# Making the x sums of a third unit of tokens in an earlier block of a fused attention and expert kernel

## The chip, the cores and the metric

One core of one Trainium2 chip. The time of a run is the device time of that core in microseconds (us), and each kernel has several runs. A profile is one execution seen by the hardware profiler; its span is about 1.7 us shorter than the time of the same execution.

## The reference, cut to what matters

Attention with cosine weights over 8 batches of 576 tokens gives x, 4608 tokens of 512 numbers. A gate matrix gives each token a weight for each of 8 experts, balanced by eight rounds of row and column sums. Each expert is a two-layer network.

```python
x = attn_out.transpose(0, 2, 1, 3).reshape(B * S, H * D)      # 4608 x 512
P = np.exp(x @ w_gate - ...)
for _ in range(8):
    P /= P.sum(1, keepdims=True); P /= P.sum(0, keepdims=True); P *= N / E
for e in range(8):
    out += P[:, e:e+1] * (np.maximum(x @ w1[e], 0) @ w2[e])
```

## The kernel before

Expert 0 runs in nine blocks of 512 tokens (block 0 to 8), mixed with the attention of the next batch. Experts 1 to 7 use a scheme of seven products in place of eight, on six units of 384 token pairs. It needs, for each unit, three sums of parts of x (S1, S2, S4) and one part of x replaced by a difference. The sums are made once and kept in DRAM; each later expert loads them again.

```python
def x_sums(n, ts):                       # unit n: four VectorE sums, three stores
    a11, a12, a21, a22 = (x_part(i, j, n) for i in range(2) for j in range(2))
    s1, s2, s4 = ts
    for out_, in0, in1, op in (
        (s1, a21, a22, ALU.add), (s2, s1, a11, ALU.subtract),
        (s4, a12, s2, ALU.subtract), (a21, a11, a21, ALU.subtract),
    ):
        ve.tensor_tensor(out=out_, in0=in0, in1=in1, op=op)
        yield
    for i, t in enumerate(ts):
        saved.append(nc.sync.dma_start(out=x_saved[n, i], in_=t...))
```

The first two units' sums are made in block 6, in tiles that the attention no longer needs (three of the k_p tiles, three of the q_p tiles); the others in expert 1, one unit ahead of their use. After block 6 the attention's tiles are given up, and H, the hidden layer's tile, takes their room. Block 7 writes into H first:

```python
for j in range(B - 1, NJ):               # blocks 7 and 8
    hT = next_h()                        # a half of H
    ...
            ffn1(hT, w0, j, [slot])      # 4 matmuls into h_ps (two buffers),
                                         # then ScalarE: relu into hT
            if j == B - 1 and slot == 0:
                gates(B - 1, Z[:])       # ScalarE: exp, start of the balancing
```

At the start of unit 1 of expert 1, two rows of the result are weighted on GpSimd:

```python
            if e == 1 and n == 0:
                ...
                w2_first(w)
                for _ in range(2):
                    gate(ungated.pop(0), nc.gpsimd)
```

Of the kernel before, what the change touches and what calls it, by code (L numbers as in the profile page):

```python
# [25 lines left out]
def kernel(  # L26
# [13 lines left out]
    B, H, S, D = q.shape  # L40
# [41 lines left out]
    def not_before(earlier, i):  # L82

        if earlier is not None:
            tc.add_manual_dep(
                i.ins,
                earlier.ins.name,
                mybir.DependencyInfo(mybir.DependencyClass.NoSync, mybir.DependencyReason.DATA),
                reason="written order",
            )  # L90
# [29 lines left out]
    def new_weights(pool):  # L120
        return pool.tile([P, KT, F], F16, name="w1e"), pool.tile([P, FT, Dm], F16, name="w2e")

    def load_w1(w, e, cuts, parts=None):
        view = moe_w1[e].rearrange("(kt p) f -> p kt f", p=P)
        for i in range(cuts) if parts is None else parts:
            f0, f1 = i * F // cuts, (i + 1) * F // cuts
            nc.gpsimd.dma_start(out=w[0][:, :, f0:f1], in_=view[:, :, f0:f1])

    def load_w2(w, e, cuts):
        view = moe_w2[e].rearrange("(ft p) d -> p ft d", p=P)  # L130
        for i in range(cuts):
            f0, f1 = i * FT // cuts, (i + 1) * FT // cuts
            nc.gpsimd.dma_start(out=w[1][:, f0:f1, :], in_=view[:, f0:f1, :])
# [61 lines left out]
    def x_sums(n, ts):  # L195
# [10 lines that stand above are left out]
            saved.append(  # L206
                nc.sync.dma_start(out=x_saved[n, i], in_=t.rearrange("p k t -> p (k t)"))
            )

    saved = []  # L210

    with ExitStack() as p1:
        ld = p1.enter_context(tc.tile_pool(name="ld", bufs=4))
        kp_pool = p1.enter_context(tc.tile_pool(name="kp_pool", bufs=4))
        qp_pool = p1.enter_context(tc.tile_pool(name="qp_pool", bufs=3))
# [419 lines left out]
        def at(block, slot, fn, *args):  # L635
            todo.setdefault((block, slot), []).append((fn, args))
# [150 lines left out]
                for half in range(2):  # L787
                    at(j, 11 + half, load, b + 2, half, "qkv", True)
        def x_sums_early(n):
            pool, name = ((kp_pool, "k_p"), (qp_pool, "q_p"))[n]  # L790
            ts = [pool.tile([P, C, 2, D], F16, name=name) for _ in range(3)]
            for _ in x_sums(n, [
                t[:].rearrange("p c a d -> p (c a d)")[:, 0 : KH * TU].rearrange(
                    "p (k t) -> p k t", k=KH
                ) for t in ts
            ]):
                pass

        for n in range(2):
            at(B - 2, (2, 5)[n], x_sums_early, n)  # L800

        y_pss = {}
        for j in range(B - 1):
# [43 lines left out]
    def next_h():  # L847
        nonlocal turns_h
        turns_h += 1
        return H[:, turns_h % 2]  # L850
# [9 lines left out]
    def x_tiles():  # L860
        return [s2_pool.tile([P, KH, TU], F16, name=name) for name in ("S1", "S2", "S4")]

    def x_again(n, ts, earlier=None):
        for i, t in enumerate(ts):
            not_before(earlier, nc.sync.dma_start(
                out=t[:].rearrange("p k t -> p (k t)"), in_=x_saved[n, i]
            ))

    def w1_sums(w, i):
        tw, steps = w1_steps(w, i)  # L870
        for step in steps:
            step()
        return tw
# [42 lines left out]
    def group(hT, tw, xs, n, i, fill):  # L916

        b11, T1, b21, b22, T2, T3, T4 = tw
        s1, s2, s4 = (t[:] for t in xs)
        h11, h12 = hT[:, i, 0:TU], hT[:, FH + i, 0:TU]  # L920
        h21, h22 = hT[:, i, TU : 2 * TU], hT[:, FH + i, TU : 2 * TU]
        X = ps_h[0].tile([P, TCH], FP32, name="h_ps")
        product(X, b11, x_part(0, 0, n), True)
        se.copy(out=Y[:, 0:TU], in_=X[:, 0:TU])  # L924
        fill()
        for fn in late:
            fn()
        late.clear()
        fill()
        product(X, T2, s2, False)  # L930
        u2 = snapshot(X, "u2")
        fill()
        product(Y, b21, x_part(0, 1, n), False)
        se.activation(out=h11, in_=Y[:, 0:TU], func=AF.Relu)  # L934
        fill()
        product(X, T1, s1, False)
        u4 = snapshot(X, "u4")
        fill()
        product(Z, T3, x_part(1, 0, n), True)
        add_relu(h22, Z, u4)  # L940
        fill()
        product(X, b22, s4, False)
        se.activation(out=h12, in_=X[:, 0:TU], func=AF.Relu)  # L943
        fill()

        def last():
            product(Z, T4, x_part(1, 1, n), False)
            add_relu(h21, Z, u2)

        late.append(last)  # L950
# [106 lines left out]
    def w2_first(w):  # L1057
        b11, b12 = w[1][:, 0:FH, 0:DH], w[1][:, 0:FH, DH:Dm]
        i = ve.tensor_tensor(out=b12, in0=b12, in1=b11, op=ALU.subtract)
        if ve is nc.vector:  # L1060
            not_before(latest, i)

    def mark(bank):

        te.matmul(
            out=bank, lhsT=xT[:, 0, 0:P], rhs=xT[:, 0, 0:TCH], start=True, stop=True,
            skip_group_check=True,
        )
# [55 lines left out]
    def gate(g, pool=None):  # L1124

        if pool is None:
            bound[2].mul(out=acc(g), in_=acc(g), mul=P_tok[:, g, 0:1])
        else:
            pool.tensor_scalar(
                out=acc(g), in0=acc(g), scalar1=P_tok[:, g, 0:1], scalar2=None, op0=ALU.mult,  # L1130
            )
# [12 lines left out]
    xs_first = [x_tiles() for _ in range(2)]  # L1144
    xs_next = xs_first[0]
# [64 lines left out]
    for e in range(1, E):  # L1210
        if e == 2:
            se = nc.scalar
        w = w_next
        for n in range(NU):
            hT = next_h()
            xs = xs_next
            for i in range(FH):
                group(hT, tws[i], xs, n, i, start_fill if e == 1 and n == 0 else pair_fill)
                m = (n + 1) % NU
                if e == 1 and m:  # L1220

                    if n == 0:
                        xs_next = xs_first[1]
                        continue
                    if i == 0:
                        xs_next = x_tiles()
                        sums_x = x_sums(m, [t[:] for t in xs_next])
                    next(sums_x)
                    if i == FH - 1:
                        next(sums_x, None)  # L1230
                elif i == 1:
                    xs_next = x_tiles()
                    if not (e == E - 1 and m == 0):
                        x_again(m, xs_next)

                if e > 1 and n == 0 and i == 0:
                    tws[FH - 1] = w1_sums(w, FH - 1)
                if e + 1 < E and n == NU - 1:
                    if i:
                        tws[i - 1] = w1_sums(w_next, i - 1)  # L1240
                    else:
                        w2_first(w_next)
            if e == 1 and n == 0:
                k_fill = 0
                for _ in balance:
                    pass
                mark(W2[:])
# [3 lines that stand above are left out]
                ve = nc.vector  # L1251
            if n == 0 and e + 1 < E:
                w_next = new_weights(wA if e % 2 else wB)
                load_w1(w_next, e + 1, 1)
            if n == 2 and e + 1 < E:
                load_w2(w_next, e + 1, 1)
            add_pairs(hT, e, w, n)
    for fn in late:
        fn()
    while stream:  # L1260
        _, pair, name = stream.pop(0)
# [32 lines left out]
```

## Time and profile before

| | us |
|---|---|
| median of 3 runs | 975.6 (975.55 to 975.99) |
| span of the profiled execution | 972.1 |
| TensorE busy | 959.4 |
| first group of block 7 starts at | 161.53 |
| from there to the end | 810.6 |

The profiled execution took 973.9 us, less than any of the three timed ones. How the views are read is told in the prediction, which shows their lines.

### The profile page before, as it was taken

What the parts mean: (1) busy time and instruction counts of PE and PEld (TensorE: products, weight loads), DVE (VectorE), ACT (ScalarE), POOL (GpSimd) and SP (SyncE); (2) the same over time, 40 slices, a digit from 0 to 9 for tenths busy, and PEclk for the clock granted to TensorE, in tenths of its full rate; (3) what the DMA queues carried; (4) which work ended last, traced back from release to release, by engine and by line L of the source; (5) the groups of instructions that cost most, each with busy time, mean ns of one, the idle gap of its engine ahead of it and who ended that gap; (6) DMA issues with size and microseconds to landing.
All of it is one profiled execution on the core that took longest, in us unless ns stands there. A gap on an engine that the chain in (4) does not pass through costs nothing.

```text
span 972.1 us, 20258 instructions
## 1 busy us (share of the span) xinstructions
PE 959.4 (99%) x7855; PEld 674.6 (69%) x7855; DVE 807.4 (83%) x1831; ACT 565.0 (58%) x1264; POOL 60.7 (6%) x82
## 2 busy tenths in 40 slices
PE   9999999999999999999999999999999999999997
PEld 6545555567777777777777777777777777777775
DVE  7767776789898887987888987987888987987887
ACT  5767665577776555555555555555555555555551
POOL 6231210010000000000000000000000000000001
PEclk9999999999999999999999999999999999999999
DMA  9999988231004301332004301322004401115435
GB/s 162 188 154 173 156 137 184 44 69 50 26 26 93 69 25 50 68 62 57 25 26 93 69 25 51 68 54 65 26 25 86 75 25 42 33 28 124 123 90 127
DMA packets 81200, 74.72 MB, mean 77 GB/s; under 512 B 33360, under 2 KB 73040, under 8 KB 81104
## 3 DMA queue, kind: packets, MB, share of 16 engines
q0 software_dynamic: 27232, 30.94, 20.4%
q1 hardware_dynamic: 53632, 42.24, 17.8%
q8 instruction: 61, 1.00, 0.4%
q14 instruction: 35, 0.29, 0.1%
q10 hardware_dynamic: 240, 0.26, 0.1%
HBM read 84.30 MB, written 12.98 MB: 100 GB/s over the span
## 4 chain that ended last, share of the span: by engine, by line
PE 91%; DMA 4%; issue 2%; DVE 1%; POOL 1%; ACT 0%; POOLq 0%; DVEq 0%; SPq 0%; ACTq 0%
PE rows_ps L109 34%; PE h_ps L109 28%; PE p_ps L109 11%; PE copied_ps L109 11%; PE y_ps L109 4%; PE small_ps L109 3%; DMA k_ld<-in_k_dram 1%; DMA w1e<-in_moe_w_dram 1%; DMA w2e<-in_moe_w_dram 1%; DVE acc_hi L975 0%; POOL q_ld L233 0%; POOL hs_last L990 0%; DMA out_dram<-acc_lo 0%; DVE H L905 0%; DVE S L203 0%
## 5 line engine op out<-in xcount | busy, mean ns | idle before, releaser
L975 DVE SCALAR_TENSOR_TENSOR acc_lo<-rows_ps,P_tok,acc_lo 128x512 f32<-128x512 f32 (+1 forms) x322 | 203.8, 642 | 74.9 <-PE rows_ps L109 74.8
L109 PEld LDWEIGHTS <-H 128*128 128x128 f16 x2080 | 203.1, 98 | 82.3 <-issue 1.4
L911 ACT CAST u<-h_ps 128x384 f16<-128x384 f32 x288 | 137.5, 478 | 129.7 <-PE h_ps L109 129.7
L109 PEld LDWEIGHTS <-w1e 128*128 128x128 f16 x1632 | 157.7, 98 | 67.2 <-issue 5.3
L905 DVE CUSTOM_DVE_ANT_0 H<-p_ps,u 128x384 f16<-128x384 f32 x329 | 181.7, 552 | 7.2 <-PE p_ps L109 7.1
L109 PEld LDWEIGHTS <-hs 128*128 128x128 f16 x1500 | 146.6, 98 | 56.2
L109 PE MATMUL p_ps<-xT,T 128*128 128x384 f16 x672 | 164.2, 326 | 1.0 <-DVE H L905 0.9
L109 PE MATMUL h_ps<-S,w1e 128*128 128x384 f16 x672 | 164.2, 326 | 0.8 <-ACT u L911 0.6
L109 PE MATMUL rows_ps<-V,H 128*128 128x256 f16 x1000 | 150.0, 273 | 0.7 <-DVE acc_hi L975 0.7
L109 PE MATMUL rows_ps<-w2e,hs 128*128 128x256 f16 x1000 | 150.0, 273 | 0.0
L109 PE MATMUL h_ps<-xT,w1e 128*128 128x384 f16 (+1 forms) x616 | 148.8, 351 | 0.1
L943 ACT ACTIVATE H<-h_ps 128x384 f16<-128x384 f32 x144 | 70.6, 490 | 94.5 <-PE h_ps L109 94.5
L109 PEld LDWEIGHTS <-T 128*128 128x128 f16 x1008 | 98.4, 98 | 31.9 <-issue 4.9
L109 PE MATMUL rows_ps<-w2e,H 128*128 128x256 f16 (+1 forms) x568 | 94.4, 285 | 0.0
L924 ACT COPY copied_ps<-h_ps 128x384 f32<-128x384 f32 x144 | 67.5, 469 | 36.0 <-PE h_ps L109 35.2
L934 ACT ACTIVATE H<-copied_ps 128x384 f16<-128x384 f32 x144 | 70.8, 492 | 20.4 <-PE copied_ps L109 20.4
L109 PE MATMUL h_ps<-S,T 128*128 128x384 f16 x336 | 81.8, 325 | 0.6 <-ACT copied_ps L109 0.5
L109 PE MATMUL copied_ps<-xT,w1e 128*128 128x384 f16 x336 | 82.1, 326 | 0.0
L109 PE MATMUL copied_ps<-w2e,H 128*128 128x256 f16 x504 | 75.6, 273 | 0.0
L109 PE MATMUL rows_ps<-V,hs 128*128 128x256 f16 x500 | 75.0, 273 | 0.0
L975 DVE SCALAR_TENSOR_TENSOR acc_lo<-copied_ps,P_tok,acc_lo 128x256 f32<-128x256 f32 x126 | 60.3, 479 | 0.4
L975 DVE SCALAR_TENSOR_TENSOR acc_hi<-rows_ps,P_tok,acc_hi 128x512 f32<-128x512 f32 (+1 forms) x56 | 41.4, 739 | 20.6 <-PE rows_ps L109 19.7
(146 smaller groups left out, 947.7 us busy)
## 6 DMA issues: line engine op xcount, KB each, us to landing
S<-x_saved SPq DMA_DIRECT2D x114, 192.0 KB, 2.4
out_dram<-acc_lo SPq DMA_DIRECT2D x62, 128.0 KB, 2.4
w1e<-in_moe_w_dram POOLq DMA_DIRECT2D x7, 1024.0 KB, 8.8
w2e<-in_moe_w_dram POOLq DMA_DIRECT2D x7, 1024.0 KB, 9.6
q_ld<-in_q_dram POOLq DMA_DIRECT2D x16, 288.0 KB, 6.5
k_ld<-in_k_dram POOLq DMA_DIRECT2D x16, 288.0 KB, 7.8
v_ld<-in_v_dram POOLq DMA_DIRECT2D x16, 288.0 KB, 9.6
x_saved<-S SPq DMA_DIRECT2D x12, 192.0 KB, 1.8
```

The lines of the kernel that those rows point to most:

```text
L109: i = getattr(self.engine, name)(*args, **kwargs)
L905: latest = ve._custom_dve(TENSOR_ADD_SAT, out=out, in0=ps[:, 0:TU], in1=t[:], s0=FP32_MAX, s1=0.0)
L911: se.copy(out=t[:], in_=ps[:, 0:TU])
L924: se.copy(out=Y[:, 0:TU], in_=X[:, 0:TU])
L934: se.activation(out=h11, in_=Y[:, 0:TU], func=AF.Relu)
L943: se.activation(out=h12, in_=X[:, 0:TU], func=AF.Relu)
L975: ve.scalar_tensor_tensor(out=a, in0=rows, scalar=P_tok[:, g, self.e : self.e + 1], in1=a, op0=ALU.mult, op1=ALU.add,)
```

## The change

Its intent: VectorE is backed up at the start of unit 1 of expert 1, where three of the four sums of the third unit stand in its queue, and idle for 3 us at the end of block 6. So the third unit's sums are made there too, stored, and loaded in expert 1 like the others.

```diff
-            pool, name = ((kp_pool, "k_p"), (qp_pool, "q_p"))[n]
+            pool, name = ((kp_pool, "k_p"), (qp_pool, "q_p"))[n % 2]
             ts = [pool.tile([P, C, 2, D], F16, name=name) for _ in range(3)]
...
-        for n in range(2):
-            at(B - 2, (2, 5)[n], x_sums_early, n)
+        for n in range(3):
+            at(B - 2, (2, 5, 9)[n], x_sums_early, n)
...
-                if e == 1 and m:
-                    if n == 0:
-                        xs_next = xs_first[1]
-                        continue
+                if e == 1 and n == 0:
+                    xs_next = xs_first[1]
+                    continue
+                if e == 1 and m > 2:
                     if i == 0:
                         xs_next = x_tiles()
...
-                        x_again(m, xs_next)
+                        x_again(m, xs_next, saved[-1] if e == 1 and m == 2 else None)
```

## The prediction

The forecast's sum is 975.6 - 0.5 + 3.1 = 978.2 us. Passages of the recorded text that no trace or run of this case shows are cut where it is marked; they are general statements (among them that a sum could be made no cheaper, which was not shown), and no term of the sum is among them.

> **What bounds the kernel now.** I read the page first, its busy times and its chain, to see which engine sets the time:
>
> ```profile
> PE 959.4 (99%) x7855; PEld 674.6 (69%) x7855; DVE 807.4 (83%) x1831; ACT 565.0 (58%) x1264; POOL 60.7 (6%) x82
> ...
> PE 91%; DMA 4%; issue 2%; DVE 1%; POOL 1%; ACT 0%; POOLq 0%; DVEq 0%; SPq 0%; ACTq 0%
> ```
>
> TensorE works 959.4 of 972.1 us and is 91% of the chain. So VectorE work has no price of its own: it costs or saves only where TensorE stands still for it. The order of instructions of the built program (not run) shows that TensorE's own order is the same, instruction by instruction, before and after. The question is only which TensorE waits go and which come. The waits of TensorE between 160 and 206 us, the stretch from block 7 to the second unit of expert 1, which are all that the change can touch:
>
> ```profile
> PE p_ps L109 <- DVE H L905: 0.9, 1, 0.9
> PE h_ps L109 <- ACT copied_ps L109: 0.5, 1, 0.5
> ```
>
> (From 206 to 300 us the same view has one wait of 0.6 us, for ScalarE.) The first line is the intended prize. The timeline of VectorE and TensorE there (start, duration, engine, operation):
>
> ```profile
> 198.91 0.74 DVE L203 TENSOR_TENSOR S<-xT 128x768 f16<-128x768 f16 x1 [0.46 <-PE h_ps L109]
> 199.69 0.56 DVE L203 TENSOR_TENSOR S<-S,xT 128x768 f16<-128x768 f16 x1
> 200.17 0.55 DVE L109 CUSTOM_DVE_ANT_0 H<-p_ps,u 128x384 f16<-128x384 f32 x1
> ...
> 201.28 0.55 DVE L203 TENSOR_TENSOR S<-xT,S 128x768 f16<-128x768 f16 x1
> ...
> 202.34 0.54 DVE L905 CUSTOM_DVE_ANT_0 H<-p_ps,u 128x384 f16<-128x384 f32 x1
> ...
> 205.02 0.55 DVE L905 CUSTOM_DVE_ANT_0 H<-p_ps,u 128x384 f16<-128x384 f32 x1
> ```
>
> VectorE is backed up; three of the four x sums of the third unit (L203, into S) stand in the queue, and the H at 205.02 lets TensorE go on only at 205.62.
>
> Now the place that receives the work, the end of block 6. VectorE there:
>
> ```profile
> 159.64 1.55 DVE L109 TENSOR_TENSOR xT<-small_ps,rb 128x384 f16<-128x384 f32 x4 [3.12 <-PE small_ps L109]
> ```
>
> An idle of 3.12 us, large enough for four sums. But the stores that follow the sums must land as well. The queue of stores and loads, and what it waits for:
>
> ```profile
> 152.37 1.51 SPq L207 DMA_DIRECT2D x_saved<-q_p  x3
> 162.62 2.76 SPq L865 DMA_DIRECT2D S<-x_saved  x6
> ```
>
> ```profile
> SPq L865 <- DMA x_saved<-q_p: 8.6, 2, 7.4
> ```
>
> The reloads wait for the stores of the second unit to land. Landing times, the instructions that touch q_p between 152.3 and 153.9 us:
>
> ```profile
> L207 SPq DMA_DIRECT2D x_saved<-q_p x3: 319/320/320, 152.4 to 153.6; - x3
> ...
> DMA to landing us min/median/max: 7.5/8.3/8.9
> ```
>
> So the last store, issued at 153.6, lands at 153.56 + 8.9 = 162.5. ScalarE's first write into the new tile H:
>
> ```profile
> 162.67 0.60 ACT L109 ACTIVATE H<-h_ps 128x512 f16<-128x512 f32 x1 [0.35 <-PE h_ps L109]
> ```
>
> It starts 0.2 us after that landing. The view names TensorE, whose matmuls (161.53, 1.03 us long) ended at 162.56, but it could not have started much earlier for the store either.
>
> [...] 768 columns take 0.55 us and the 1152-column products of the same kind 0.75, that is 384 more columns in 0.20 us, 1.9 a nanosecond. [...]
> [...] the six stores, issued from 147.9 to 153.6, land one after another, the last four at 158.6, 159.9, 161.2 and 162.5 (issue plus landing delay, same view for each), 1.3 us apart, while the weight loads of expert 1, issued at 147.15 and 147.90, run beside them. A store without that company (at 199.7 us) takes 1.9 us.
> [...]
>
> **The change part by part.**
> Removed in expert 1, unit 1: four sums (three of them before 205 us), three stores. I walked the new VectorE order with the old durations, from start to next start. The reciprocal and the gate product end at 198.46 as before. H (p_ps ready at 199.45) starts at 199.45 instead of 200.17; then its own 0.47, w2e 0.65, V 0.68, acc_hi 0.59 bring the H of 202.34 to 201.85. Up to the next H stand V, hs, V, H and hs, 0.47 + 0.61 + 0.33 + 0.61 + 0.33 + 0.34 = 2.69 later, at 204.54 instead of 205.02: the new order puts another V between, so of the 1.9 us removed only 0.48 reach this H. TensorE's wait shrinks from 0.85 to about 0.4. After that point TensorE has no wait for VectorE to lose. Saved: 0.5 us.
>
> Added in block 6: four sums of 0.59 + 0.59 + 0.48 + 0.46 = 2.1 us from 156.55 to 158.7 in the idle that lasts until 159.64. Two of them need k_p buffers that the stores of the first unit read, landed at 153.8 and 157.0; the sum that needs the second starts at about 157.7. No cost on VectorE.
>
> Added: three stores of 192 KB, issued at about 157.2, 157.8 and 158.4, in the same ring behind the q_p stores, of which the last lands at 162.5. In the built program, ScalarE's first write into H waits, before and after, for all stores out of k_p and q_p, because H takes their room in SBUF; after, the wait's counts include the three new stores. At 1.28 us each they land at about 163.8, 165.1 and 166.3; I take 166.1, since the weight load ends meanwhile and the ring then has the engines to itself.
> The write into H then starts at 166.1 + 0.15 = 166.25 instead of 162.67. TensorE can run two groups ahead, for h_ps has two buffers. The third group starts at 163.76 now (within 162.89 and 1.89 for eight matmuls) and would start when the first buffer is free, 166.25 + 0.6 = 166.85. New TensorE wait: 3.1 us. Nothing later gives it back, TensorE being busy to the end.
> Also added: three reloads in unit 1 of expert 1, some 15 us before their use; hidden. The six reloads of the first two units move from 162.6 into the time after the stores and land by about 171, needed at about 185.9; hidden.
>
> Sum: 975.6 - 0.5 + 3.1 = 978.2 us.
>
> **The rivals.**
> A: the stores land in time and the intended saving stands alone: 975.1 us. For it: VectorE has room, and unhindered stores take 1.9 us. Against: the measured 7.5 to 8.9 us for stores issued just before into the same ring.
> B: the new stores share bandwidth better than I think, because the bulk of the q_p stores is through by 161 us and only stragglers land at 162.5. Then the third lands at about 165.0, the wait is 2.0 us, the time 977.1.
> C: the stores slow the load of w2 so far that it or the reloads hold up unit 0 of expert 1. It lands 17.4 us after 147.9, at 165.3; its use is at 200. There are 35 us of room: no change of the time.
> D: the Sinkhorn chain slips. ScalarE's exponentials for it stand just behind the write into H, so they move by 3.6 us while TensorE moves by 3.1; the chain has 0.9 us before TensorE needs its first column sums (ready 165.45, used 166.34). It holds, but narrowly; at worst some 0.5 us more.
> E: removing sums helps all of unit 1 by their full 2.1 us: 973.5. Against: TensorE waits for VectorE there once, for 0.85 us.
>
> **Range and chances.** The mechanism (a wait for the new stores) is in the program; its size hangs on the third landing, between 165.0 (B) and 167. That gives 977.1 to 979.1, with some room below for A: 976.4 to 979.2. Two per cent would be 19.5 us, far outside all of this.
>
> **What would show it.** Right: a TensorE wait of about 3 us in the group h_ps at 163.8, put down to ScalarE (or ScalarE idle about 3.5 us before its first H), with the last x_saved<-k_p landing at about 166; the wait at 205.6, shifted, at about 0.4. Wrong: stores out of k_p landing before 163.5, no such wait, and a time below 975.6; or a wait of 0.85 gone entirely, which would make my walk of the VectorE order too pessimistic.

## The result, and the profile after

| | before | after |
|---|---|---|
| median, us | 975.63 (975.55 to 975.99, 4 runs) | 983.46 (980.55 to 984.02, 4 runs) |
| span of the profile | 972.1 | 981.2 |
| first group of block 7 | 161.53 | 163.76 |
| from there to the end | 810.6 | 817.4 |

The ratio of the fast runs is 1.0074 (95% interval 1.0053 to 1.0094): within 2%, but slower, and outside the predicted range. A ratio here is the mean time of one kernel's fast runs over the mean of the other's in the same rounds, so not quite the ratio of the medians.

The busy times and the chain of the page of the kernel after, which answer to the first lines of the prediction:

```profile
PE 963.5 (98%) x7855; PEld 676.0 (69%) x7855; DVE 807.6 (82%) x1831; ACT 565.3 (58%) x1264; POOL 61.1 (6%) x82
...
PE 90%; DMA 4%; DVE 3%; ACT 1%; issue 1%; POOL 1%; SPq 0%; POOLq 0%; DVEq 0%
```

TensorE is busy 4.1 us longer though it does the same instructions in the same order, and the span is 9.1 us longer. So some of its work became slower, and some of its time became idle. TensorE's waits between 160 and 225 us:

```profile
PE h_ps L109 <- ACT H L109: 3.7, 1, 3.7
PE p_ps L109 <- DVE H L905: 0.8, 1, 0.8
PE h_ps L109 <- ACT copied_ps L109: 0.5, 1, 0.5
```

The first is new; the second, which the change was to take away, is still there. The timelines of TensorE and then of ScalarE around the new wait:

```profile
165.13 1.02 PE L109 MATMUL h_ps<-xT,w1e 128*128 128x512 f16 x4
169.86 5.28 PE L109 MATMUL h_ps<-xT,w1e 128*128 128x512 f16 x12 [3.71 <-ACT H L109]
```

```profile
169.22 0.60 ACT L109 ACTIVATE H<-h_ps 128x512 f16<-128x512 f32 x1 [4.67 <-DMA S<-x_saved]
```

ScalarE's first write into H waits 4.67 us, and TensorE, its two h_ps buffers full, waits with it. Then 12 matmuls take 5.28 us, 0.44 each, where the same ones took 0.22 each before. The windows view (columns: stretch, its length, busy time and count of TensorE, weight loads, VectorE, ScalarE, GpSimd, granted clock, DMA share, GB/s):

```profile
166.00:169.86 3.86, 0.15 (x1) 0.00 (x0) 0.00 (x0) 0.64 (x3) 0.00 (x0) 0.84 1.12 337
169.86:175.54 5.68, 5.68 (x16) 2.29 (x15) 2.58 (x7) 2.09 (x5) 0.00 (x0) 0.51 0.13 49
175.54:181.00 5.46, 5.46 (x28) 2.60 (x27) 4.86 (x14) 2.62 (x5) 0.00 (x0) 1.00 0.02 3
```

The granted clock is 0.51 for the 5.7 us after the wait. The profile's whole-kernel clock, 0.996 against 0.999, hides it, and so do the page's 40 slices of 25 us. Stretches of the same view, cut where the clock changes, show that it was halved for 6.83 us, from 168.64 to 175.47, and so already before the wait ended:

```profile
165.22:168.64 3.42, 0.93 (x7) 0.30 (x4) 0.00 (x0) 0.00 (x0) 0.00 (x0) 1.00 1.15 297
168.64:172.05 3.41, 2.19 (x6) 0.79 (x6) 2.00 (x5) 1.47 (x4) 0.00 (x0) 0.50 0.61 225
172.05:175.47 3.42, 3.42 (x11) 1.50 (x10) 0.50 (x3) 1.20 (x3) 0.00 (x0) 0.50 0.00 0
```

The label of ScalarE's wait is wrong and shows how such labels mislead. It names the reloads into S, but the first of them, issued at 164.9, landed at 169.7, after ScalarE had started. The new stores, as the instructions that touch k_p from 158.9 to 160.6 us show them:

```profile
L207 SPq DMA_DIRECT2D x_saved<-k_p x3: 319/319/320, 159.2 to 160.4; - x3
...
DMA to landing us min/median/max: 6.8/7.6/8.2
```

The last lands at 160.43 + 8.2, at 168.67 by the trace, half a microsecond before the write into H.

Following each TensorE matmul from the one profile into the other (the counts are equal) splits the 8.8 us by which the last one is later: 2.2 arise before the end of block 1, that is before anything that the change touches; 3.9 at the new wait; 2.7 in the slow matmuls after it; and 0.0 at unit 1 of expert 1, where 0.5 was to be won. The other 0.3 us of the 9.1 lie after the last matmul: from its end to the end of the span it is 4.03 to 4.06 us in the three profiles without more stores (before, e1, e6), and 4.33 to 4.37 in the eight comparable ones with three more. Why was not looked for.

### The profile page after: what moved, and what is told of

Same layout as the page of the kernel before. It is cut to its first block, busy times and chain, and to the rows that moved or that the text cites. A ratio compares the mean times of both kernels' runs of the same rounds, so it can differ in the third digit from the quotient of the medians.

```text
span 981.2 us, 20264 instructions
## 1 busy us (share of the span) xinstructions
PE 963.5 (98%) x7855; PEld 676.0 (69%) x7855; DVE 807.6 (82%) x1831; ACT 565.3 (58%) x1264; POOL 61.1 (6%) x82
## 4 chain that ended last, share of the span: by engine, by line
PE 90%; DMA 4%; DVE 3%; ACT 1%; issue 1%; POOL 1%; SPq 0%; POOLq 0%; DVEq 0%
PE rows_ps L109 34%; PE h_ps L109 27%; PE p_ps L109 11%; PE copied_ps L109 11%; PE y_ps L109 4%; PE small_ps L109 3%; DMA q_pT<-q_p 1%; DMA x_saved<-q_p 1%; DMA k_ld<-in_k_dram 1%; DMA acc_hi<-q_p 1%; ACT hT L109 0%; DMA S<-x_saved 0%; DVE den L109 0%; DVE q_p L109 0%; DVE acc_hi L975 0%
## 5 line engine op out<-in xcount | busy, mean ns | idle before, releaser
L109 PE MATMUL h_ps<-xT,w1e 128*128 128x384 f16 (+1 forms) x616 | 151.6, 355 | 3.8 <-ACT H L109 3.7
```

Of the source, the lines that this page charges most:

```text
L109: i = getattr(self.engine, name)(*args, **kwargs)
```

## The experiments

My theory after this: the stores make ScalarE's write into H wait, the idle time halves TensorE's clock, and the 2.2 us at the start are chance. Rivals: the sums in block 6, the reloads, or the stores' traffic cost by themselves; the slow matmuls come from those transfers and not from idle time; the late start belongs to the change. The column "block 7 to end" is the span less the start of the first group of block 7, both of the one profile.

| run | median of timed runs, us | first group of block 7 | block 7 to end |
|---|---|---|---|
| before | 975.63 | 161.53 | 810.6 |
| after | 983.46 | 163.76 | 817.4 |
| e1, before again | 974.99 (one run) | 162.74 | 810.6 |
| e2, other room | 974.71 | 166.72 | 810.3 |
| e3, wait filled with 14 matmuls | 979.83 | 163.57 | 814.8 |
| e4, w2 loaded later | 975.45 | 162.84 | 810.8 |
| e5, stores alone | 981.08 | 168.28 | 816.3 |
| e6, sums alone | 975.94 | 163.56 | 810.6 |
| e7, other room, gates on ScalarE | 975.39 | 163.56 | 810.1 |
| e8, wait filled with 6 matmuls | 979.60 | 163.16 | 814.7 |
| e9, other room, gates after V | 976.79 | 165.45 | 811.0 |
| e10, other room again | 975.99 | 164.12 | 810.4 |
| e11, after again | 981.62 | 164.15 | 816.4 |

The kernel before, run beside them, had medians of 976.32 (974.80 to 977.71, 11 runs, beside e1 to e4), 975.35 (974.65 to 976.63, 9 runs, e5 to e8) and 975.95 (975.26 to 976.58, 9 runs, e9 to e11). All results were correct. Where no ratio is given below, it is 1.0049 (1.0026 to 1.0072) for e3, 1.0067 (1.0040 to 1.0093) for e5, 1.0005 (0.9991 to 1.0019) for e6 and 1.0043 (1.0029 to 1.0057) for e8.

### e1_before_again: the kernel before, unchanged

> The kernel before, unchanged, for one more profile. In the profile after, TensorE was already 2.2 us later by the start of block 2, long before anything that the change touches. If that is chance of the start (my theory), this profile may begin its block 7 (first h_ps group) anywhere between 161.5 us, as in the profile before, and 164 us, and the time is 975 to 976 us with it. If the 2.2 us belong to the change, this profile stands at 161.5 again.

Block 7 starts at 162.74, 1.2 us later than in the first profile of the same program, and the rest takes the same 810.6 us. So the start varies without any change. In the twelve later profiles block 7 starts between 162.74 and 168.28, and two profiles of one kernel differ too (e2 and e10, 166.72 and 164.12). The first profile of before was an early one. Its two starts are still the earliest of all, so these profiles alone do not exclude that a few tenths belong to the change; but the ratios of e2, e4, e6 and e10 to before, 0.9995 to 1.0005, show nothing of the kind.

### e2_other_room: the third unit's sums where H does not lie

```diff
+            if n == 2:        # room of the v tiles, free since slot 2 of block 6
+                room = [lent[:, i * KH * TU : (i + 1) * KH * TU] for i in range(3)]
+                for _ in x_sums(n, [r.rearrange("p (k t) -> p k t", k=KH) for r in room]):
+                    pass
+                return
```

> The changed kernel with the third unit's three sums in the room of the v tiles (free since slot 2 of block 6) in place of k_p tiles, so that H does not lie over them; same sums, same stores, same reloads. Theory (ScalarE's first write into H waits for the three new stores, and TensorE then runs at half clock for a while): no wait at block 7, no half clock, 975.1 to 975.7 us, 0 to 0.5 us under before. Rival (the stores' traffic, the sums in block 6 or the reloads cost by themselves): above 978 us as in the changed kernel.

Ratio to before 1.000 (0.998 to 1.002). The stores are as slow as in the changed kernel (the instructions that touch x_saved from 162 to 163.6 us; the view calls the lent room acc_lo), and the wait at block 7 is gone (TensorE's waits from 150 to 225 us):

```profile
L207 SPq DMA_DIRECT2D x_saved<-acc_lo x3: 320/320/320, 162.2 to 163.4; - x3
...
DMA to landing us min/median/max: 6.9/7.6/8.3
```

```profile
PE p_ps L109 <- DVE H L910: 0.8, 1, 0.8
PE h_ps L109 <- ACT copied_ps L109: 0.2, 1, 0.2
```

The same sums, stores and reloads cost nothing that the ratio shows once TensorE does not have to wait for the stores. That refutes the rivals of traffic, sums and reloads, and with them the label that named the reloads. Two of its six runs took 978.8 and 979.2 us, the other four 974.4 to 974.8. The profiled one is of the slow two, and its loss lies in block 1, which all these kernels share: TensorE waits 3.5 us for a transposing transfer (waits from 66 to 82 us), and its clock is halved after that too:

```profile
PE small_ps L109 <- DMA acc_hi<-q_p: 3.5, 1, 3.5
```

```profile
75.80:79.00 3.20, 3.19 (x13) 1.17 (x13) 2.54 (x5) 0.60 (x1) 0.00 (x0) 0.50 1.20 203
```

### e3_filled and e8_half_filled: matmuls without purpose in the wait

```diff
+            if j == B - 1 and slot == 1:
+                for i in range(14):          # 6 in e8_half_filled
+                    te.matmul(out=Y[:], lhsT=xT[:, 0, 0:P], rhs=xT[:, 0, 0:TCH], ...)
```

> The changed kernel with 14 matmuls of 512 columns into an unused bank (3.0 us at full clock) in TensorE's wait at block 7. Theory (after 3.7 us without work TensorE gets half its clock for some 5 us, which costs 2.7 us): the wait left is 0.7 to 1.2 us, the clock stays full, time 979.5 to 981 us, 2.5 to 3.5 us under the changed kernel. Rival (the slow matmuls come from something else than the idle time, such as the reloads that land at the same time): as the changed kernel, 983 us or more.

> The changed kernel with 6 matmuls (1.3 us) in place of 14 in the wait at block 7. It leaves about 2.5 us without work. Theory (the clock is halved only by an idle time as long as the 3.7 us of the changed kernel, not by any): full clock after it, 979.5 to 981 us apart from the start, the same as with 14. Rival (any idle of over some 1 to 2 us halves it): half clock after the wait as in the changed kernel, 982 us and more.

With 14, TensorE still waits 0.8 us; with 6, 2.5 us. In both the clock stays at 1.00 through every window from 166 to 178 us, and both take about 4.2 us more than before from block 7 on, against 6.8 for the changed kernel. The two are alike, as they must be if the end of the wait is set by the stores. So the other 2.7 us are the price of the long idle time, for the same transfers run in all three. The line of e8 for the stretch after its wait:

```profile
169.00:172.00 3.00, 2.70 (x14) 1.37 (x14) 2.45 (x6) 2.02 (x5) 0.00 (x0) 1.00 0.36 134
```

That e8's 2.5 us kept the full clock does not make every wait of 2.5 us safe: in the changed kernel the clock was halved 2.5 us after TensorE's last matmul (its end at 166.15, the change at 168.64). What else the traces show of this is told under the failed step below.

### e4_w2_later: the weight load out of the stores' way

```diff
-    w_next = load_weights(wB, 1)
+    w_next = new_weights(wB)
+    load_w1(w_next, 1, 1)
...
+            if j == B - 1 and slot == 5:
+                load_w2(w_next, 1, 1, se.last)      # after ScalarE's sixth write into H
```

> The changed kernel with the load of expert 1's second weight issued only after the sixth write into H of block 7, so the stores have the DMA engines to themselves after the first weight load. Theory (the stores land late since they share with the weight loads): the last store lands 2 to 4 us after its issue, before ScalarE's first H is due; no TensorE wait over 0.5 us at block 7; 975.1 to 975.9 us. Rival (the landing is late by the ring's own order and write time, without the loads): a wait of over 2 us and a time above 978 us.

The last of the new stores now lands 3.2 us after its issue, all by 162.7 us (instructions that touch k_p, 158.2 to 159.7 us):

```profile
DMA to landing us min/median/max: 3.2/3.3/3.4
```

TensorE's waits from 150 to 225 us show none at block 7:

```profile
PE p_ps L109 <- DVE H L908: 0.8, 1, 0.8
PE h_ps L109 <- ACT copied_ps L109: 0.5, 1, 0.5
```

The ratio is 0.9995 (0.9983 to 1.0007). So it was the load of w2 beside them that made the stores land late: 6.8 to 8.2 us after their issue with it, 3.2 to 3.4 without.

### e5_stores_alone and e6_sums_alone: half of the change each

```diff
+        def stores_again():                  # e5: stores of unit 0's sums, to a spare tensor
+            for i, t in enumerate(kept):
+                saved.append(nc.sync.dma_start(out=x_spare[i], in_=t))
+                after(ve.last, saved[-1])
+        at(B - 2, 9, stores_again)
```

```diff
+            for _ in range(4):               # e6: four sums that nobody reads, in block 6
+                ve.tensor_tensor(out=t, in0=x_part(1, 0, 2), in1=x_part(1, 1, 2), op=ALU.add)
```

> The kernel before, with three more stores of 192 KB alone, out of the first unit's k_p tiles into a spare tensor, issued after the second numerators of block 6; sums, reloads and unit 1 of expert 1 as before. Theory (the stores alone make the loss, through ScalarE's wait at H and the half clock after it): a TensorE wait of 3 to 4 us at the third h_ps group of block 7, half clock after it, 981 to 984 us apart from the chance of the start, that is 6 to 7 us more than before from block 7 to the end. Rival (VectorE's sums in block 6 or the changed order in expert 1 cost as well): clearly less than the changed kernel's 6.6 us, under 4 us.

> The kernel before, with four more sums of 768 columns alone in block 6, into a k_p tile that nobody reads; no more stores. Theory: they lie in VectorE's idle time, no wait at block 7, the same time as before from block 7 to the end within 0.2 us. Rival (VectorE is late for block 7): at least 1 us more.

The stores alone cost 5.7 us from block 7 on, a little under the 6 to 7 that I expected: the wait is 3.6 us in the profile, and the half clock after it costs 1.6 in place of 2.7, for it lasts 3.41 us (174.20 to 177.61) in place of 6.83. (Its profile is also one with a late start, a 3.4 us wait in block 1 with half clock after it, 0.50 from 76 to 82 us.) TensorE's waits of e5 from 60 to 225 us, the first two:

```profile
PE h_ps L109 <- ACT H L109: 3.6, 1, 3.6
PE small_ps L109 <- DMA acc_hi<-q_p: 3.4, 1, 3.4
```

The sums alone cost nothing; they lie in the idle time before the numerators, as the prediction had it (VectorE's timeline):

```profile
158.47 2.32 DVE L109 TENSOR_TENSOR k_p<-xT 128x768 f16<-128x768 f16 x4
161.67 1.55 DVE L109 TENSOR_TENSOR xT<-small_ps,rb 128x384 f16<-128x384 f32 x4 [0.88 <-PE small_ps L109]
```

### e7_gates_on_scalar and e9_gates_after_v: where the saving went

In the kernel after, VectorE's V at the start of unit 1 took longer than the 0.68 us that I had walked with, while GpSimd made its two weighted rows (timelines of VectorE and of GpSimd; GpSimd's spans are rough):

```profile
208.88 0.68 DVE L109 TENSOR_TENSOR w2e<-w2e 128x1024 f16<-128x1024 f16 x1
209.60 1.06 DVE L1007 TENSOR_TENSOR V<-w2e 128x1024 f16<-128x1024 f16 x1
```

```profile
207.41 3.58 POOL L1129 TENSOR_SCALAR acc_lo<-acc_lo,P_tok 128x512 f32<-128x512 f32 x2 [13.91 <-DVE P_tok L109]
```

Both experiments start from e2.

```diff
-                    gate(ungated.pop(0), nc.gpsimd)      # e7: ScalarE in place of GpSimd
+                    gate(ungated.pop(0))
```

```diff
                     v2 = ve.tensor_tensor(out=tw2[0], in0=b22, in1=b12, op=ALU.subtract)
+                    while first_gates:                   # e9: GpSimd, but only after V
+                        after(v2, gate(first_gates.pop(0), nc.gpsimd))
```

> The kernel with the third unit's sums in the other room, and the two gate products that GpSimd makes at the start of unit 1 of expert 1 given to ScalarE. The V after w2e took 1.06 us there in place of the 0.68 that I had walked with, beside GpSimd's 3.6 us. Theory (GpSimd's products stretch VectorE's beside them, which ate the saving): V takes 0.68 again and the next H comes 0.4 us earlier against TensorE; the wait there falls to 0.3 to 0.5 us, unless ScalarE's two products (0.73 each) hold up TensorE by as much. Rival (V is long for another reason, such as its operands' place): V still takes about 1.06 us.

> The kernel with the other room, GpSimd's two gate products held back until the first V is made, so that V runs alone and the products lie beside the later V, hs and H sums, all of them with two inputs in SBUF. If the stretching was tied to that one V, it takes 0.68 us and the wait at the next H falls to 0.4 to 0.5 us, 0.4 us less from block 7 to the end than in the other-room kernel (that is about 0.9 to 1.0 us less than before). If GpSimd's products stretch whatever two-input sum of VectorE runs beside them (my theory since the run with the gates on ScalarE), some later sum takes 0.3 to 0.5 us longer instead and the wait stays at about 0.8 us.

With the gates on ScalarE, V takes 0.69 us and TensorE's wait for VectorE's H is gone altogether. ScalarE's two products cost TensorE 0.8 us just before it; followed matmul by matmul against the profile before, TensorE loses 0.8 and gains 1.0, so 0.2 us net in that unit. With GpSimd's products after V, V takes 0.69 us, but two later sums of half its width, hs, are stretched instead, while GpSimd makes its two products (206.01 to 210.00, rough; VectorE's timeline of e9; a third hs, unstretched, takes 0.41):

```profile
204.39 0.69 DVE L1012 TENSOR_TENSOR V<-w2e 128x1024 f16<-128x1024 f16 x1
...
206.68 1.04 DVE L995 TENSOR_TENSOR hs<-H 128x512 f16<-128x512 f16 x1
...
208.58 0.82 DVE L995 TENSOR_TENSOR hs<-hs,H 128x512 f16<-128x512 f16 x1
```

The wait grew to 1.5 us: one stretch of 0.38 became two of 0.63 and 0.41. So in these runs the slow sums are ones beside GpSimd's products, and not always that one V. Neither kernel shows it in its median: e7's ratio is 1.0001 (0.9987 to 1.0014), e9's 1.0009 (0.9996 to 1.0021).

### e10_other_room_again and e11_after_again

> The other-room kernel again, on a new chip allocation, as the best version so far: its first six runs fell into two groups, four at 974.4 to 974.8 and two at 978.8 to 979.2 us, the latter (the profiled one) with a late start. Theory: the late start is a matter of the run and not of the kernel; from block 7 to the end it is again 0.3 to 0.6 us shorter than before, and most of its runs are at 974 to 976 us. Rival: its slow runs come from its own stores or room; then a late part shows after block 7.

> The changed kernel again, for a second profile and on the same chip as the other-room kernel. Theory: from block 7 to the end 5.4 to 6.8 us more than before; the wait is again 3.6 to 3.9 us, and the half clock after it costs 1.5 to 2.8 us, as it varied between the changed kernel and the one with the stores alone. Rival: the 2.2 us of late start come again, exactly as in the first profile, which would make them the change's own.

The other-room kernel is again equal to before (0.9999, 0.9987 to 1.0012), and now its runs lie together, 975.5 to 976.5. From block 7 on it is 0.2 to 0.3 us shorter in both profiles. That gain does not lie where the change works: by following the matmuls, it comes in two steps of 0.28 us (at about 190 us of the kernel before and at 740), both where TensorE waits for ScalarE to copy a bank; why they vanish with the other room stays open. The two steps make 0.56 us; the 0.3 us more after the last matmul take half of it back.
The changed kernel is slower again: 1.0056 (1.0028 to 1.0083). Its second profile has the same wait, 3.6 us, and 1.7 us of slow matmuls, with the half clock from 170.39 to 173.81, 3.41 us. Its late start, 2.6 us this time, arises in other waits than in the first profile and is of the size that kernels without the change show as well. Some 1.5 us of it are half clock too, in block 1, from 61.17 to 64.58 us, after no wait of TensorE longer than 1.75 us, but after a stretch in which TensorE was busy for less than half (the windows view):

```profile
57.75:61.16 3.41, 1.61 (x11) 0.69 (x8) 0.88 (x3) 2.10 (x5) 0.00 (x0) 1.00 1.20 151
```

## Why the prediction was wrong

- The direction and the mechanism were right: a TensorE wait in the group h_ps at block 7, put there by stores out of k_p landing at about 166 us. Counted without the 2.2 us of late start, the last landed at 166.4 (predicted 166.1). e2, e4 and e5 show the mechanism by three different edits. Of the prediction's rivals, A, B, C and E are refuted; the slip that D foresaw was not seen in any run.
- The size of the wait was off: "starts at 166.1 + 0.15" measured 0.55 after the landing. The instructions of ScalarE between 168.6 and 169.22 us show seven semaphore checks, one after another, in the half microsecond from the landing at 168.67 to the write at 169.22; the first starts at 168.69, and in the built program it is the one for the last new store:

```profile
L109 ACTq EVENT_SEMAPHORE  x7: 17/38/38, 168.7 to 169.1; - x7
```

  In the kernel before, the write came 0.2 us after the last store's landing, but TensorE's matmuls too ended only 0.1 us before it. Landing 0.3 later and checks 0.4 longer make the 3.1 us into 3.8, of the 3.9 by which TensorE's third group came later.
- The step that failed is "New TensorE wait: 3.1 us. Nothing later gives it back, TensorE being busy to the end." I priced an idle time of TensorE at its own length. In all three profiles with it (after, e11, e5) an idle time of 3.6 to 3.7 us also took half the clock from what followed, for 6.83, 3.41 and 3.41 us, which cost 2.7, 1.7 and 1.6 us. This term was absent from the sum, and at 2.7 it alone would have put the prediction at 980.9, above the range.
- The traces show more of this term, but not what sets it. The clock changes at 168.64 and 175.47 in the first profile of the changed kernel, at 61.17, 64.58, 170.39 and 173.81 in e11, and at 174.20 and 177.61 in e5; within each profile these lie 3.41 us or a whole multiple of it apart (6.83 is twice that, and the 105.8 from 64.58 to 170.39 is 31 times). In the 3.41 us before a fall, TensorE was busy for this share: 0.27 at the wait of the changed kernel, 0.08 in e11 and 0.00 in e5; in block 1, 0.47 in e11, 0.34 in e5 and 0.03 in e2. The first profiles of the kernels before and after, cut into stretches of 3.41 us in step with their changes, have no stretch of under 0.57 that full clock followed (0.57 is at 974.20 in the one after). But a stretch cut anywhere does not tell: with waits of 2.5 us in e8 and 2.7 in e9 the clock stayed at 1.00, though from 166.00 to 169.00 TensorE was busy for 0.84 us in e8, and from 73.00 to 76.00 for 0.33 in e9. So the length of a wait did not decide alone; that its place among the stretches decides with it is my reading and was not tested. The cost differs between runs of the same wait: 3.41 us of half clock in e5 and e11, 6.83 in the first profile of the changed kernel. It can also be missed: one of the eight timed runs of the changed kernel (e11, 978.09 us) and two of e5's four have a mean clock of 0.999, which leaves no room for 3.41 us of half clock before the kernel's end. That one run lies within the predicted range, by luck: the prediction did not have the term.
- "Saved: 0.5 us" was wrong: 0.0. I walked VectorE's new order with durations from a stretch of the old one in which GpSimd worked beside other instructions. After the change V stood beside GpSimd and took 1.06 us in place of 0.68. Counted without the 8.83 us by which all stood later there, the H that I had walked to 201.85 came at 202.35: the H before it started 0.13 later than walked, w2e took 0.07 more from start to start, and V 0.30 more. With no GpSimd product beside it V took 0.69 us (e7, e9). Not every sum beside GpSimd was stretched: in the kernel after, w2e took 0.68 us though it started 1.5 us into GpSimd's two products of 3.6 us together, and the stretched sums lost 0.38 to 0.63 us. GpSimd's pair took 3.1 us in the kernel before, 3.6 after and 4.0 in e9 (GpSimd's spans are rough). Why some were stretched and others not is not shown.
- The sum with the measured terms of the first profile is 975.6 + 3.9 + 2.7 - 0.0 = 982.2, or 982.5 with the 0.3 us after the last matmul. The median after is 983.5 in the first series, and 5.7 us above before in the second. What is left, about 1 us either way, is of the size of the start's variation and of 3.41 us of half clock more or less (1.6 to 1.7 us); which of them it was is not shown.

## What to carry to other kernels

Before you move work into idle time, ask also who next writes over its buffers: here the write into H waited for a store's landing at 168.67, 8.2 us after its issue, and not for the issue. The new stores landed after 6.8 to 8.3 us beside the load of w2 (3.2 to 3.4 with that load moved away), where a store at 199.7 us of the kernel before took 1.9. Price an idle time of TensorE by its length and by the clock after it: waits of 3.6 to 3.7 us cost 1.6 to 2.7 us more here. The length alone did not tell whether the clock fell: it stayed at 1.00 with waits of 2.5 us (e8) and 2.7 us (e9), and in e11 it fell after no wait longer than 1.75 us. With the empty matmuls of e3 and e8 in the wait it stayed. Durations measured beside one neighbour did not carry over to another (V: 0.68 us as walked, 1.06 beside GpSimd): look at what GpSimd does while VectorE's sums run.
